# Attention with decay into a tanh MLP on one core: bulk loads unheld, first q copied at once, an early MLP start in slot 4, and unread matmuls in slots 0 to 3

## The chip, the cores and the metric

The kernel runs on 1 core of one Trainium2 chip. The metric is the device time of one execution in microseconds; the time quoted is the median of several runs.

## The reference

The attention has 8 batches, 8 heads, 576 tokens and head size 64. Its result, with the 8 heads side by side (512 channels), goes row by row through a two-layer MLP of width 2048.

```python
scores = scale * np.matmul(q, k.transpose(0, 1, 3, 2))
cum = np.cumsum(np.log(np.clip(f, 0.0001, 1.0)), axis=-1)
decay = cum[:, :, :, None] - cum[:, :, None, :]
scores = np.where(causal, -1000000000.0, scores + decay)
attn = softmax(scores)                       # over the last axis
x = np.matmul(attn, v).transpose(0, 2, 1, 3).reshape(B * S, H * D)
h = x @ w_in
out = (h - np.tanh(h)) @ w_out               # float32, 4608 x 512
```

## The kernel before, in words

**Slots.** The 64 heads are worked as 32 pairs (two heads of one batch, four pairs a batch). Slot p computes the scores of pair p, the values of pair p-1, and turns the result of pair p-2 or p-1 into the transposed layout XR (channels by tokens) that the MLP reads. `att_items(p)` writes out a slot: seven score tiles (`TILES`, numbered ti 0 to 6), and between them transposes of the next pair's q and k (`trans`, line 232, for batches 0 to 2; later batches are transposed by DMA), loads (`LOADS`, keyed by slot and tile), `values` (line 325 and the division L332 to L334) and `turn`. `turn` goes over TensorE and a ScalarE copy (L345, L346) in batch 0 and over two DMA transposes on SyncE's queue (L348, L350) in the others.

**The MLP** works on 9 blocks u of 512 tokens, each of 16 steps `mlp1` (hidden tile ft: four matmuls over the channel quarters ci, Tanh on ScalarE, the sum on VectorE; L360, L363, L366) and 16 steps `mlp2` (four matmuls each, L374; every fourth ends with a ScalarE copy and a store, L378 and L380). Channel quarter ci is pair ci of a batch. The list `mlp` of 288 steps is handed out to the slots, `take` of them to each (none in slots 0 to 3, then 2, 8, 7, 7, 7, 7, and 8 from slot 10 on), spread among a slot's items after the first `first` items; the remaining steps run behind slot 32.

**Scores.** A tile is a matmul of KT by QT over 64 rows of head dimension and 3 rows that add the decay: chi and clo (the scaled cumulative sum in two halves, rows of KT) and cq (a row of QT). These rows are put in place by DMA (`load_aug`). In the first pair, tiles 0 to 2 add the decay by two extra matmuls instead (`decay_part`, L263 and L265, from `dec`, `sel` and `cq`), so that they need no row from a DMA. Exp runs on ScalarE (L303). In batch 0 the causal mask is a further matmul (L297), in the others a GpSimd select (L313).

**The order of the work.** Inside `tc.manual_schedule` the instructions of TensorE, GpSimd, SyncE and VectorE run in the order in which the program writes them; ScalarE's order is left to a scheduler. Loads of q, k, v and the weights are issued on GpSimd's queue; decay rows, DMA transposes and stores mostly on SyncE's.

**The start.** q and k of heads 0 to 3 are loaded first, f gives lf (clip L140, Ln L148), cum (scan L150), chi (L153) and clo (L157). `start()` issues 33 unread matmuls (L389: products of a constant tile that nothing reads), transposes the first q and k, copies them out of PSUM (four ScalarE copies L243, four VectorE copies L245, two of each left over for `later()`), calls `load_aug(0)`, then `bulk()`, which loads heads 4 to 7 of q and k and the rest of v for batch 0. Ahead of that load stands `hold`: VectorE writes one column of clo into a place of qn that the load overwrites, so the load can't be issued before clo is there (L173).

**PSUM pools.** `ps_sc` has two buffers for score tiles, `ps_av` one for values, `ps_m` three (MLP, early transposes, `turn` of batch 0), `ps_tr` one (late transposes, score tile 3 in batch 0, and the unread matmuls).

Of the kernel before, what the change touches and what calls it, by code (L numbers as in the profile page):

```python
# [21 lines left out]
def kernel(  # L22
# [10 lines left out]
    nc = tc.nc  # L33
    P = 128

    B, H, S, D = q.shape
    NH = B * H
# [3 lines left out]
    NPAIR = H // 2  # L41
# [5 lines left out]
    NCH = DM // P  # L47
    UW = 512
    NU = NT // UW

    cst = ctx.enter_context(tc.tile_pool(name="cst", bufs=1))
# [9 lines left out]
    ps_tr = ctx.enter_context(tc.tile_pool(name="ps_tr", bufs=1, space=PSUM))  # L61
    ps_m = ctx.enter_context(tc.tile_pool(name="ps_m", bufs=3, space=PSUM))
# [61 lines left out]
    minus16 = cst.tile([2 * H, S], FP16)  # L124
    nc.vector.memset(minus16, -1.0)
    nc.vector.memset(sel, 0.0)
    nc.vector.memset(sel[0:1, 0:UW], -1.0)
    nc.vector.memset(sel[NH:NH + 1, 0:UW], -1.0)
    nc.vector.memset(sel[0:1, UW:UW + P], 1.0)
    nc.vector.memset(dec[:, S:PITCH], 0.0)  # L130
# [4 lines left out]
    late = cst.tile([P, P], FP16)  # L135
    nc.vector.memset(late, 0.0)
# [3 lines left out]
    nc.vector.tensor_scalar(out=lf, in0=lf, scalar1=0.0001, scalar2=1.0,  # L140
                            op0=ALU.max, op1=ALU.min)
    def clean(i, eng):
        eng.memset(KT[i][:, :, S:PITCH], 0.0)
        eng.memset(vn[i][D:P, NJ - 1, :, :], 0.0)
        eng.memset(vn[i][:, :, :, D:VW], 1.0)

    clean(0, nc.vector)
    nc.scalar.activation(out=lf, in_=lf, func=AF.Ln)  # L148
# [10 lines left out]
    def load_aug(b):  # L159
        i, hs = b % 2, slice(b * H, (b + 1) * H)  # L160
        nc.sync.dma_start(out=KT[i][D:D + 1, :, 0:S], in_=chi[hs, :])
        (nc.gpsimd if b == 0 else nc.sync).dma_start(out=QT[i][D + 2:D + 3, :, :], in_=cq[hs, :])
        nc.sync.dma_start(out=KT[i][D + 1:D + 2, :, 0:S], in_=clo[hs, :])

    def const_rows(i):
# [2 lines left out]

    const_rows(0)

    def hold(dst, *at):
        spot = dst[0][(slice(0, NH),) + at]
        nc.vector.tensor_copy(out=spot, in_=clo[:, 0:1])  # L173

    def bulk():
        hold(qn, 4, 0, slice(0, 1))
        load_qk(qn, q, 0, 4, H)
        load_qk(kn, k, 0, 4, H)
        for n in range(NJ - 1):
            load_v_block(0, n, 2, H)  # L180
# [156 lines left out]
    def turn(b, c):  # L337
        xn = XN.pop((b, c))
        r0 = b % 4 * S
        if b == 0:  # L340
            x32 = ps_m.tile([P, UW], FP32, tag="m", name="x32")
            xt = x32.bitcast(FP16)[:, 0:S]
            for ib in (NJ - 1, 0, 1, 2, 3):
                w0 = min(ib * P, S - P)
                nc.tensor.transpose(out=xt[:, w0:w0 + P], in_=xn[:, ib, :], identity=id16)  # L345
            nc.scalar.activation(out=XR[:, c, r0:r0 + S], in_=xt, func=AF.Copy)  # L346
            return
        nc.sync.dma_start_transpose(out=XR[:, c, r0:r0 + S - D].rearrange("p (n t) -> p n t", t=P),  # L348
                                    in_=xn[:, 0:NJ - 1, :].rearrange("p n d -> p (n d)"))
        nc.sync.dma_start_transpose(out=XR[:, c, r0 + S - D:r0 + S], in_=xn[D:P, NJ - 1, :])  # L350

    def mlp1(u, ft):
        hps = ps_m.tile([P, UW], FP32, tag="m", name="hps")
        t0 = u * UW % RING
        parts = [(0, t0, min(UW, RING - t0))]
        if t0 + UW > RING:
            parts.append((RING - t0, 0, t0 + UW - RING))
        for o, t, n in parts:
            for ci in range(NCH):
                nc.tensor.matmul(out=hps[:, o:o + n], lhsT=win[:, ci, ft * P:(ft + 1) * P],  # L360
                                 rhs=XR[:, ci, t:t + n], start=(ci == 0), stop=(ci == NCH - 1))
        th = tmp.tile([P, UW], FP32, tag="th", name="th")
        nc.scalar.activation(out=th, in_=hps, func=AF.Tanh, scale=-1.0)  # L363
        gt = gtp.tile([P, UW], FP16, tag="gt", name="gt")
        GT[(u, ft)] = gt
        nc.vector.tensor_tensor(out=gt, in0=hps, in1=th, op=ALU.add)  # L366
# [12 lines left out]
            r0 = u * UW + m * P  # L379
            nc.sync.dma_start(out=out[r0:r0 + P, :], in_=ost)  # L380

    IDLE = []

    def unread(n):
        if not IDLE:
            IDLE.append(ps_tr.tile([P, UW], FP32, tag="tr", name="idle"))
        idle = IDLE[0]
# [3 lines left out]
    pairs = [(b, c) for b in range(B) for c in range(NPAIR)]  # L391

    def start():
        unread(33)
        rest = trans(*pairs[0], qn, QT, True, "AAAA", True)
        nc.scalar.activation(out=cq, in_=cum, func=AF.Copy, bias=-SHIFT * inv_qscale, scale=inv_qscale)
        nc.scalar.activation(out=expo, in_=lf[0:1, 0:1], func=AF.Exp)
        load_aug(0)
        unread(6)
        rest += trans(*pairs[0], kn, KT, True, "VVVV", True)  # L400
        bulk()
        unread(12)
        decay(0)
        unread(8)
        REST.extend(rest)

    REST = []

    def later():
        for fn in REST:  # L410
# [10 lines left out]
    def att_items(p):  # L421
        def put(fn, *args):
            items.append((lambda: fn(*args), True))

        items = []
        here = pairs[p] if p < len(pairs) else None
        before = pairs[p - 1] if 0 < p <= len(pairs) else None
        after = pairs[p + 1] if p + 1 < len(pairs) else None
        early = p < NPAIR
        if p == 0:  # L430
            put(start)
        for ti in range(len(TILES)):
            if here:
                put(scores, *here, ti)
            if p == ti == 0:
                put(later)
            if p == 1 and ti == 3:
                put(last)
            for load in LOADS.get((p, ti), ()):
                items.append((load, False))  # L440
            if ti == 0 and after and after[0] < FAR:
                put(trans, *after, qn, QT, early, "VV")
            if ti == (1 if early else 3) and after and after[0] < FAR:
                put(trans, *after, kn, KT, early, "VV")
            if early and ti in (2, 3) and before:
                put(values, *before, (ti - 2,))
            elif not early and ti == 2 and before:
                put(values, *before)
            if p < NPAIR:
                if ti == 1 and p > 1:  # L450
                    put(turn, *pairs[p - 2])
            elif p == NPAIR and ti in (1, 5):
                put(turn, *pairs[p - 2 + (ti == 5)])
            elif p > NPAIR and ti == 3:
                put(turn, *before)
        return items

    mlp = [(fn, u, s) for u in range(NU) for fn in (mlp1, mlp2) for s in range(NFT)]
    at = 0
# [47 lines left out]
```

## Time and profile before

| what | value |
|---|---|
| median of 3 runs | 361.09 us (356.47 to 362.28) |
| the profiled execution: its time, its span | 361.41 us, 359.7 us |
| mean granted TensorE clock in the span | 0.986 |
| TensorE busy | 348.2 us, 97% |
| ScalarE, VectorE, GpSimd busy | 219.0, 197.4, 156.1 us |
| HBM read, written | 36.85 MB, 9.44 MB |
| share of TensorE in the chain that ended last | 86% |

How to read it: the span is what the profiler saw of one execution, the time is what the device reports for it. PE is TensorE's matmuls, PEld its weight loads, DVE VectorE, ACT ScalarE, POOL GpSimd, SP SyncE; SPq and POOLq are their instruction queues. L232 is line 232 of the kernel. The granted clock is a share of TensorE's full clock. Busy shares are means over the whole span; what a stage is worth is read from that stage.

### The profile page before, as it was taken

To read this page: it belongs to the slowest core of one execution; us is meant where nothing else is said; L and a number is where in the kernel's file an instruction comes from. 1 tells how busy PE (TensorE), PEld (TensorE's weight loads), DVE (VectorE), ACT (ScalarE), POOL (GpSimd) and SP (SyncE) were. 2 spreads that over 40 slices of the span, in tenths; PEclk is the share of its full clock that TensorE was granted. 3 is DMA by queue.
4 is the path that set the end of the run, shared out by engine and by line. 5 is a ranking of instruction groups with operands and counts; after the bars stand their busy time and mean duration, and the time that the engine had idled before them with its cause. 6 is when DMAs were issued, how large, how long until landed. Compare 5 with 4: busy or idle time off the path is not lost.

```text
span 359.7 us, 7576 instructions
## 1 busy us (share of the span) xinstructions
PE 348.2 (97%) x2833; PEld 194.3 (54%) x2833; DVE 197.4 (55%) x348; ACT 219.0 (61%) x417; POOL 156.1 (43%) x317
## 2 busy tenths in 40 slices
PE   7798999999999999999999999999999999999995
PEld 6486555555455555555557865555555544444442
DVE  8768897458871577157714681477137513802710
ACT  6559786467755785578557865786468634714611
POOL 7882743765376627662767267732222210000000
PEclk9859999999999999999999999999999999999999
DMA  9999999999499969997999999991320031011011
GB/s 109 133 206 193 181 186 141 141 130 163 70 82 179 164 93 80 170 154 116 76 127 190 112 73 142 150 156 18 91 67 13 19 88 61 2 58 58 2 48 69
DMA packets 140712, 38.74 MB, mean 108 GB/s; under 512 B 128084, under 2 KB 134980, under 8 KB 140676
## 3 DMA queue, kind: packets, MB, share of 16 engines
q0 software_dynamic: 92416, 18.37, 62.8%
q1 hardware_dynamic: 48260, 19.90, 28.4%
q8 instruction: 22, 0.36, 0.4%
q14 instruction: 14, 0.11, 0.1%
HBM read 36.85 MB, written 9.44 MB: 129 GB/s over the span
## 4 chain that ended last, share of the span: by engine, by line
PE 86%; DVE 5%; ACT 3%; DMA 3%; issue 1%; POOL 0%; POOLq 0%; ACTq 0%
PE ops L374 33%; PE hps L360 32%; PE ps L294 11%; PE av L325 8%; ACT e L303 3%; DMA kn<-in_k_dram 2%; DMA XR<-xn 1%; PE t L232 1%; DVE gt L366 1%; DVE KT L245 1%; PE ps L297 0%; DVE xn L334 0%; DVE QT L245 0%; ACT XR L346 0%; DVE cum L150 0%
## 5 line engine op out<-in xcount | busy, mean ns | idle before, releaser
L366 DVE TENSOR_TENSOR gt<-hps,th 128x512 f16<-128x512 f32 x144 | 98.5, 689 | 94.5 <-ACT th L363 93.7
L360 PE MATMUL hps<-XR,win 128*128 128x512 f16 (+1 forms) x640 | 140.2, 357 | 0.4 <-DVE gt L366 0.3
L374 PE MATMUL ops<-wout,gt 128*128 128x512 f16 x576 | 138.2, 379 | 0.0
L303 ACT ACTIVATE e<-ps 128x512 f16<-128x512 f32 x192 | 110.5, 598 | 27.6 <-PE ps L294 20.5
L363 ACT ACTIVATE th<-hps 128x512 f32<-128x512 f32 x144 | 86.7, 602 | 33.6 <-PE hps L360 31.0
L313 POOL TENSOR_SCALAR_AFFINE_SELECT e<-e 128x128 f16<-128x128 f16 x168 | 56.7, 338 | 87.7 <-ACT e L303 85.1
L360 PEld LDWEIGHTS <-win 128*128 128x128 f16 x640 | 58.0, 97 | 50.1 <-issue 1.3
L374 PEld LDWEIGHTS <-gt 128*128 128x128 f16 x576 | 52.2, 97 | 54.3
L294 PE MATMUL ps<-QT,KT 67*128 67x64 f16 (+5 forms) x384 | 78.3, 282 | 2.2 <-ACT e L303 1.7
L294 PEld LDWEIGHTS <-KT 67*128 67x128 f16 (+1 forms) x384 | 37.5, 99 | 37.6 <-issue 2.8
L378 ACT ACTIVATE ost<-ops 128x512 f32<-128x512 f32 x36 | 21.5, 596 | 50.8 <-PE ops L374 49.0
L325 PEld LDWEIGHTS <-e 128*128 128x128 f16 x896 | 33.4, 99 | 6.4 <-POOL e L313 0.7
L325 PE MATMUL av<-vn,e 128*128 128x65 f16 x896 | 34.9, 195 | 0.6 <-POOL e L313 0.6
L105 POOL DMA_DIRECT2D vn<-in_v_dram x32 | 27.9, 876 | 7.2 <-DMA win<-in_moe_w_in_dram 4.1
L334 DVE TENSOR_TENSOR xn<-av,rs 128x640 f16<-128x640 f32 x32 | 26.4, 825 | 1.1
L332 DVE TENSOR_SCALAR rs<-av 128x10 f32<-128x10 f32 x32 | 5.2, 162 | 34.9 <-PE av L325 34.6
L245 DVE COPY QT<-t 64x576 f16<-64x576 f16 x22 | 17.6, 802 | 10.9 <-PE t L232 10.7
L86 POOL DMA_DIRECT2D qn<-in_q_dram x25 | 21.4, 856 | 2.7 <-issue 2.7
L86 POOL DMA_DIRECT2D kn<-in_k_dram x25 | 21.1, 845 | 2.6 <-issue 2.6
L303 ACT ACTIVATE el<-ps 128x128 f16<-128x128 f32 x32 | 8.8, 276 | 21.6 <-PE ps L294 21.2
L313 POOL TENSOR_SCALAR_AFFINE_SELECT el<-el 128x128 f16<-128x128 f16 x28 | 8.3, 297 | 28.3 <-ACT el L303 28.1
L245 DVE COPY KT<-t 64x576 f16<-64x576 f16 (+1 forms) x26 | 19.4, 748 | 1.2 <-PE t L232 0.9
(62 smaller groups left out, 137.4 us busy)
## 6 DMA issues: line engine op xcount, KB each, us to landing
out_dram<-ost SPq DMA_DIRECT2D x36, 256.0 KB
vn<-in_v_dram POOLq DMA_DIRECT2D x24, 128.0 KB, 5.5
qn<-in_q_dram POOLq DMA_DIRECT2D x20, 128.0 KB, 3.7
kn<-in_k_dram POOLq DMA_DIRECT2D x20, 128.0 KB, 4.8
win<-in_moe_w_in_dram POOLq DMA_DIRECT2D x2, 1024.0 KB, 12.9
wout<-in_moe_w_out_dram POOLq DMA_DIRECT2D x2, 1024.0 KB, 11.6
XR<-xn SPq DMA_TRANSPOSE x56
vn<-in_v_dram POOLq DMA_DIRECT2D x12, 64.0 KB, 4.9
```

Source lines behind the costliest of these rows:

```text
L86: nc.gpsimd.dma_start(out=dst[b % 2][0:pn, n, :].rearrange("p (h d) -> p h d", h=H), in_=src[b, :, n * P:n * P + pn, :].rearrange("h p d - ...
L105: nc.gpsimd.dma_start(out=vn[b % 2][:, n, h0:h1, 0:D], in_=v[b, h0:h1, n * P:(n + 1) * P, :].rearrange("h p d -> p h d"))
L245: nc.vector.tensor_copy(out=to, in_=of)
L294: nc.tensor.matmul(out=ps[:, col:col + n], lhsT=KT[b % 2][0:rows, h, j * P:(j + 1) * P], rhs=QT[b % 2][0:rows, h, i0:i0 + n], start=not ow ...
L303: nc.scalar.activation(out=e[:, lo:hi], in_=ps[:, lo:hi], func=AF.Exp, scale=qscale)
L313: nc.gpsimd.affine_select(out=view, in_=view, compare_op=ALU.is_ge, fill=0.0, base=0, pattern=pat, channel_multiplier=-1)
L325: nc.tensor.matmul(out=av[:, a, ib, :], lhsT=E.pop((b, c, a, j, ib)), rhs=vn[b % 2][:, j, 2 * c + a, 0:D + 1], start=(j == 0), stop=(j == ib))
L334: nc.vector.tensor_tensor(out=xn.rearrange("p i (a d) -> p a i d", a=2), in0=av[:, :, :, 0:D], in1=rs.to_broadcast([P, 2, NJ, D]), op=ALU. ...
L360: nc.tensor.matmul(out=hps[:, o:o + n], lhsT=win[:, ci, ft * P:(ft + 1) * P], rhs=XR[:, ci, t:t + n], start=(ci == 0), stop=(ci == NCH - 1))
L363: nc.scalar.activation(out=th, in_=hps, func=AF.Tanh, scale=-1.0)
L366: nc.vector.tensor_tensor(out=gt, in0=hps, in1=th, op=ALU.add)
L374: nc.tensor.matmul(out=ops, lhsT=GT[(u, ft)][:, m * P:(m + 1) * P], rhs=wout[:, ft, :], start=(ft == 0), stop=(ft == NFT - 1))
```

## The change

Five groups of edits:

- **Start chain.** Of the two one-row memsets of -1 in `sel`, the one in row 64 becomes a ScalarE Copy (scale -1) of a row of ones. The memsets of `late` and of the end of `dec` move ahead of the remaining ones, and in `clean` the memset of KT moves behind those of vn. All of `start()` is now in written order on ScalarE too: two q copies, then cq, then Exp's first use, and the two other q copies between score tiles.
- **Bulk loads.** `hold` is gone, so `bulk()` depends on nothing. The cq row of batch 0 is loaded on SyncE's queue.
- **Slots 0 to 3.** `unread(3)` follows score tiles 0, 1, 2, 5 and 6. `unread` takes a new tile from `ps_tr` at each call; the call with 12 in the start now has 22. Score tiles 0 and 1 of the first pair are part of `start()`, and the transposes of pair 1 move to tiles 1 (q) and 3 (k) of slot 0.
- **Slot 4.** `turn` of pair 2 follows tile 0; after tile 1 come the values of pair 3, then three `mlp1` steps over channel quarters 0 to 2 alone, then the turn of pair 3 (through `ps_tr`); their last quarter, Tanh and sum follow tiles 2 to 4. Its transposes move to tiles 2 and 4.
- **Handing out.** The three steps leave the list; slots take 2 (slot 4), 7 (5 to 7), 6 (slot 8) and 8 (from slot 9 on).

```diff
-    nc.vector.memset(sel[NH:NH + 1, 0:UW], -1.0)
+    nc.scalar.activation(out=sel[NH:NH + 1, 0:UW], in_=ones16[0:1, 0:UW], func=AF.Copy, scale=-1.0)
...
     def load_aug(b):
-        (nc.gpsimd if b == 0 else nc.sync).dma_start(out=QT[i][D + 2:D + 3, :, :], in_=cq[hs, :])
+        nc.sync.dma_start(out=QT[i][D + 2:D + 3, :, :], in_=cq[hs, :])
...
-    def hold(dst, *at):
-        spot = dst[0][(slice(0, NH),) + at]
-        nc.vector.tensor_copy(out=spot, in_=clo[:, 0:1])
-
     def bulk():
-        hold(qn, 4, 0, slice(0, 1))
         load_qk(qn, q, 0, 4, H)
...
-            x32 = ps_m.tile([P, UW], FP32, tag="m", name="x32")
+            x32 = (ps_tr if c == NPAIR - 1 else ps_m).tile([P, UW], FP32, tag="tr" if c == NPAIR - 1 else "m", name="x32")
...
-    def mlp1(u, ft):
-        hps = ps_m.tile([P, UW], FP32, tag="m", name="hps")
+    HP = {}
+
+    def mlp1(u, ft, part=None):
+        if part != 1:
+            HP[(u, ft)] = ps_m.tile([P, UW], FP32, tag="m", name="hps")
+        hps = HP[(u, ft)]
...
-            for ci in range(NCH):
+            for ci in {None: range(NCH), 0: range(NCH - 1), 1: (NCH - 1,)}[part]:
...
+        if part == 0:
+            return
...
     def start():
         unread(33)
-        rest = trans(*pairs[0], qn, QT, True, "AAAA", True)
+        q_rest = trans(*pairs[0], qn, QT, True, "AAAA", True)
...
         load_aug(0)
         unread(6)
-        rest += trans(*pairs[0], kn, KT, True, "VVVV", True)
+        k_rest = trans(*pairs[0], kn, KT, True, "VVVV", True)
         bulk()
-        unread(12)
+        unread(22)
         decay(0)
         unread(8)
-        REST.extend(rest)
...
+        scores(*pairs[0], 0)
+        for fn in k_rest:
             fn()
+        q_rest[0]()
+        scores(*pairs[0], 1)
+        q_rest[1]()
...
-            if here:
+            if here and (p > 0 or ti > 1):
                 put(scores, *here, ti)
+            if early and ti in (0, 1, 2, 5, 6):
+                put(unread, 3)
...
-            if ti == 0 and after and after[0] < FAR:
+            at_q, at_k = (1, 3) if p == 0 else (0, 1) if early else (2, 4) if p == NPAIR else (0, 3)
+            if ti == at_q and after and after[0] < FAR:
                 put(trans, *after, qn, QT, early, "VV")
-            if ti == (1 if early else 3) and after and after[0] < FAR:
+            if p == NPAIR and ti > 1 and ti < 5:
+                put(mlp1, 0, ti - 2, 1)
+            if ti == at_k and after and after[0] < FAR:
                 put(trans, *after, kn, KT, early, "VV")
-            if early and ti in (2, 3) and before:
+            if p == NPAIR:
+                if ti == 0:
+                    put(turn, *pairs[p - 2])
+                elif ti == 1:
+                    put(values, *before)
+                    for ft in range(3):
+                        put(mlp1, 0, ft, 0)
+                    put(turn, *before)
+            elif early and ti in (2, 3) and before:
...
-    with tc.manual_schedule(engines={PE, mybir.EngineType.Pool, mybir.EngineType.SP, mybir.EngineType.DVE}):
+    with tc.manual_schedule(engines=FOUR | {mybir.EngineType.Activation}):
+        start()
+    with tc.manual_schedule(engines=FOUR):
...
-            take = 0 if p < NPAIR else 2 if p == NPAIR else 7 if NPAIR + 1 < p <= 2 * NPAIR + 1 else 8
+            take = 0 if p < NPAIR else 2 if p == NPAIR else 7 if p < 2 * NPAIR else 6 if p == 2 * NPAIR else 8
-            first = 10 if p == NPAIR else 0 if p == NPAIR + 1 else 0
+            first = 16 if p == NPAIR else 0
```

More of the change, by code (lines that the diff above doesn't have):

```diff
@@ L126 @@
     nc.vector.memset(sel, 0.0)
+    late = cst.tile([P, P], FP16)
+    nc.vector.memset(late, 0.0)
+    nc.vector.memset(dec[:, S:PITCH], 0.0)
     nc.vector.memset(sel[0:1, 0:UW], -1.0)
-    nc.vector.memset(sel[NH:NH + 1, 0:UW], -1.0)
     nc.vector.memset(sel[0:1, UW:UW + P], 1.0)
-    nc.vector.memset(dec[:, S:PITCH], 0.0)
+    nc.scalar.activation(out=sel[NH:NH + 1, 0:UW], in_=ones16[0:1, 0:UW], func=AF.Copy, scale=-1.0)
     EL = [cst.tile([P, 192], FP16, tag=f"el{i}", name=f"el{i}") for i in range(3)]
@@ L134 @@
     load_v_head(0, 1)
-    late = cst.tile([P, P], FP16)
-    nc.vector.memset(late, 0.0)
     nc.gpsimd.affine_select(out=late, in_=late, compare_op=ALU.is_ge, fill=-60000.0,
@@ L142, in clean @@
     def clean(i, eng):
-        eng.memset(KT[i][:, :, S:PITCH], 0.0)
         eng.memset(vn[i][D:P, NJ - 1, :, :], 0.0)
         eng.memset(vn[i][:, :, :, D:VW], 1.0)
+        eng.memset(KT[i][:, :, S:PITCH], 0.0)
     clean(0, nc.vector)
@@ L380, in mlp2 @@
             nc.sync.dma_start(out=out[r0:r0 + P, :], in_=ost)
-    IDLE = []
     def unread(n):
-        if not IDLE:
-            IDLE.append(ps_tr.tile([P, UW], FP32, tag="tr", name="idle"))
-        idle = IDLE[0]
+        idle = ps_tr.tile([P, UW], FP32, tag="tr", name="idle")
         for i in range(n):
@@ L391 @@
     pairs = [(b, c) for b in range(B) for c in range(NPAIR)]
+    REST = []
     def start():
         unread(33)
-        rest = trans(*pairs[0], qn, QT, True, "AAAA", True)
+        q_rest = trans(*pairs[0], qn, QT, True, "AAAA", True)
         nc.scalar.activation(out=cq, in_=cum, func=AF.Copy, bias=-SHIFT * inv_qscale, scale=inv_qscale)
@@ L399, in start @@
         unread(6)
-        rest += trans(*pairs[0], kn, KT, True, "VVVV", True)
+        k_rest = trans(*pairs[0], kn, KT, True, "VVVV", True)
         bulk()
-        unread(12)
+        unread(22)
         decay(0)
         unread(8)
-        REST.extend(rest)
-    REST = []
-    def later():
-        for fn in REST:
-            fn()
+        scores(*pairs[0], 0)
+        for fn in k_rest:
+            fn()
+        q_rest[0]()
+        scores(*pairs[0], 1)
+        q_rest[1]()
         for e in EL[0:2]:
@@ L429, in att_items @@
         early = p < NPAIR
-        if p == 0:
-            put(start)
         for ti in range(len(TILES)):
-            if here:
+            if here and (p > 0 or ti > 1):
                 put(scores, *here, ti)
-            if p == ti == 0:
-                put(later)
+            if early and ti in (0, 1, 2, 5, 6):
+                put(unread, 3)
             if p == 1 and ti == 3:
@@ L451, in att_items @@
                     put(turn, *pairs[p - 2])
-            elif p == NPAIR and ti in (1, 5):
-                put(turn, *pairs[p - 2 + (ti == 5)])
             elif p > NPAIR and ti == 3:
@@ L458 @@
     mlp = [(fn, u, s) for u in range(NU) for fn in (mlp1, mlp2) for s in range(NFT)]
+    mlp = mlp[3:]
     at = 0
-    with tc.manual_schedule(engines={PE, mybir.EngineType.Pool, mybir.EngineType.SP, mybir.EngineType.DVE}):
+    FOUR = {PE, mybir.EngineType.Pool, mybir.EngineType.SP, mybir.EngineType.DVE}
+    with tc.manual_schedule(engines=FOUR | {mybir.EngineType.Activation}):
+        start()
+    with tc.manual_schedule(engines=FOUR):
         for p in range(len(pairs) + 1):
```

## The prediction

> **What bounds the kernel now.** I read the page first: busy time and slices, then the chain.
>
> ```profile
> PE 348.2 (97%) x2833; PEld 194.3 (54%) x2833; DVE 197.4 (55%) x348; ACT 219.0 (61%) x417; POOL 156.1 (43%) x317
> PE   7798999999999999999999999999999999999995
> PEclk9859999999999999999999999999999999999999
> PE 86%; DVE 5%; ACT 3%; DMA 3%; issue 1%; POOL 0%; POOLq 0%; ACTq 0%
> ```
>
> TensorE sets the end nearly everywhere. From about 40 us it is full at full clock, and no edit removes work there. Room is left only in the first slices, where TensorE is less busy and the third slice has half the clock. Second view: the first 40 us in stretches of 1 us (busy time of PE, PEld, DVE, ACT, POOL, then granted clock, DMA share, GB/s).
>
> ```profile
> 9.00:10.00 1.00, 1.00 (x15) 0.62 (x12) 0.92 (x4) 0.45 (x2) 0.51 (x1) 1.00 0.09 15
> 10.00:11.00 1.00, 1.00 (x9) 0.34 (x6) 0.97 (x4) 0.43 (x1) 1.00 (x3) 1.00 0.23 41
> ...
> 15.00:16.00 1.00, 0.59 (x7) 0.24 (x4) 0.79 (x2) 0.96 (x3) 1.00 (x2) 0.94 2.31 158
> 16.00:17.00 1.00, 0.00 (x0) 0.00 (x0) 0.80 (x1) 0.23 (x1) 0.17 (x1) 0.50 2.39 154
> ...
> 26.00:27.00 1.00, 1.00 (x27) 0.88 (x25) 0.66 (x2) 0.10 (x1) 0.16 (x1) 0.94 1.11 211
> ```
>
> The reader sees an unused DMA at 9 to 11 us, an empty TensorE at 16 us, and the half clock from 15.88 to 26.12 (0.94 is 12% of a microsecond at half). Third: the timelines of GpSimd and TensorE name the cause.
>
> ```profile
> 9.49 0.71 POOL L80 DMA_DIRECT2D qn<-in_q_dram  x1 [1.25 <-DVE qn L173]
> 10.18 0.67 POOL L80 DMA_DIRECT2D kn<-in_k_dram  x1
> ...
> 17.03 0.66 PE L232 MATMUL t<-id,kn 96*128 96x96 f16 x6 [1.44 <-DMA kn<-in_k_dram]
> ```
>
> The held load of k is issued at 10.18 and lands 6.8 us later, while TensorE stands for 1.44 us. The slots (one head pair each) begin with their first 512-wide score matmul at 9.25, 14.46, 22.01, 28.32 and 32.94 (slot 4), and slot 5 at 39.35. The change must bring slot 4's start and slot 4 itself forward.
>
> **The change, part by part.**
>
> *Start chain.* One memset (3.48 to 4.02, 0.54 us) leaves VectorE's queue ahead of the clip, the scan and the first scores. ScalarE writes that row by a Copy ahead of Ln. Here is the unknown:
>
> ```profile
> 0.81 1.28 ACT L148 ACT_TABLE_LOAD   x1 [0.81 <-PEq L491]
> 4.61 0.68 ACT L148 ACTIVATE lf<-lf 64x576 f32<-64x576 f32 x1 [2.52 <-DVE lf L140]
> 5.31 1.28 ACT L397 ACT_TABLE_LOAD   x1
> ```
>
> Loads stand where a function first needs one, so the Copy, now first, may get a load of its own and push Ln's behind it: memset of sel done 2.70, Copy about 0.6, load 1.28, Ln 4.63 to 5.31, against 5.29 now. Then the scan comes 0.1 us earlier instead of 0.54. I take 0.1 (ends 0 and 0.54), so the first scores start at 9.15. The q copies move ahead of cq and of Exp's load; that load then ends near 8.9, before the first Exp near 9.75. If the scores came 0.9 us earlier it would be late.
> The Trainium skill (ScalarE: Activation LUTs, Table sets: the hidden batching unit) says that cheap functions are in every set as filler; by that alone Ln's set could serve the Copy and the gain would be 0.54. No run so far has a Copy before Ln.
>
> *Bulk loads.* Without the hold GpSimd goes on at 7.36 (end of its select L137) instead of 9.49, 2.1 us earlier; the DMA share from 9 to 12 is 0.35, so 3 x 0.65 = 1.95 us of transfer time lie unused there. I take 1.8: k lands at 15.2. TensorE will reach the transposes that need it at about 15.9 (below): the 1.44 us wait goes. The first half of win, landing at 29.98, comes at 28.2; slot 4 will want it near 30.5, so it stays covered. The cost: batch 0's three decay rows (SyncE, 0.66 us of issue each, cq's now also there, so 7.2 to 9.2) share the engines with bulk traffic. The rows of batch 1, issued 10.09 to 12.17 beside bulk traffic, have their packets on the engines up to 16, up to 4.4 us after issue. So the last row lands by 13; the fourth tile of slot 0 wants it at about 12.7. I take 0.2 us of loss (ends 0 and 1.5).
>
> *Unread matmuls.* Ten more in the start are covered by the wait for clo (now 1.2 us). In slots 0 to 3 there are 15 each at 0.058 us (12 take 0.70 us at full clock): 0.87 us. What hides them: slot 3, at full clock, lasts 4.62 us, and its TensorE timeline stands for 0.23 + 0.63 + 0.15 = 1.0 us, because ScalarE (0.27 to 0.6 per exponential plus 0.65 for XR) and VectorE (1.61 + 1.62 + 0.17 + 0.22 + 0.83 = 4.45 us) set the pace. Uncovered they would cost 0.87 us a slot. Their tile has one buffer, shared with the fourth score tile, so the fourth group waits for that tile's Exp; the scores just ahead already wait for an earlier Exp, hence nothing.
> What they buy is the clock. It rises between the transposes at 4.83 (0.66 us for six, half rate) and at 5.79 (0.42), falls at 15.88 and rises at 26.12: steps of 10.24 us. I count columns times rows/128 from TensorE's timeline. Whole steps don't separate (10431 before the fall, 8309 before the rise), thirds do: those before a full clock have 3352 (22.70 to 26.12) or more, those before a half clock 2735 (12.47 to 15.88) or less. Fifteen unread matmuls add 1920 columns a slot, about 1400 a window: 4100. The clock then holds.
> The Trainium skill (TensorE: Matmul & The Clock Gate, Why this matters for your kernels) asks only for no idle gap over about 3 us; the trace fell after 0.3 us of idling inside a 1.44 us gap, so it disagrees. By the rule the clock would owe nothing to the unread matmuls, and they would be a cost of up to 4 x 0.87 us, near rival 2's time.
>
> *Slots 0 to 3, summed.* Slot 0 lasts 5.21 us, of it 0.50 waiting for ScalarE; plus 0.87 less 0.50 gives 5.6 (the two q copies moved in here cost ScalarE 1.0 us, in 2.2 us that it stands there now): slot 1 at 14.75, its k transposes near 15.9. Three slots at 4.65 (slot 3's pace): slot 4 at 28.7 instead of 32.94. Gain 4.2 us, the start chain's 0.1 within it.
>
> *Slot 4.* It takes 6.41 us now. Its work at full clock: two MLP pieces 1.74, values 0.91, two turns 0.56, transposes 0.52, scores 1.38, together 5.1; 1.3 us is waiting for XR, VectorE and ScalarE. The three part-pieces (9 matmuls, 1.94 us) lie just where values' division (1.3 us) must be waited for. Three more whole pieces are done here, work and not gain. ScalarE then has 7.7 us in a slot of about 8, so I take 1.0 (ends 0.3 and 1.3).
>
> *Given back at slot 9.* The MLP is two steps further on, so the first piece of token block 1, which needs pair 7's XR, comes first in slot 9. Now:
>
> ```profile
> 73.98 1.29 SPq L348 DMA_TRANSPOSE XR<-xn  x1
> ...
> 77.67 1.24 PE L360 MATMUL hps<-XR,win 128*128 128x512 f16 x4
> ```
>
> The transfer takes 4.50 us in the chain and costs TensorE 0.2 us. From the last value matmul (71.78) it is issued after 2.2 us, or 1.55 where no store is ahead (pair 6: 62.85, 64.39): landing after 6.05. TensorE gets there after 0.2 + three MLP steps of 0.865 + scores 0.72 + transposes 0.26 + 0.65 of the piece = 4.45. Wait 1.6, 0.2 of it there already; I take 1.2 net (ends 0 and 1.6). What is late next: nothing, the other engines catch up. At the later blocks five steps lie between (about 6.1 us), nothing by the same landing.
>
> **Sum.** 4.2 - 0.2 + 1.0 - 1.2 = 3.8 us off the profiled execution's own 361.41 (its span 359.7 and 1.7 around it): 357.6. That execution is 0.3 above the median 361.09, so 357.3.
>
> **Rivals.**
> 1. *More gain.* Ln is not pushed back (0.45 more), the transfer lands in time at slot 9 (1.2), slots at VectorE's 4.5 us (0.45), slot 4 full (0.3): 354.9. For it: each is an end above, and one run of 356.47 exists. Against: VectorE and ScalarE must interlock perfectly.
> 2. *The clock falls all the same* in slots 1 to 3: 10.24 us at half rate, where a slot's 8094 columns (scores 3200, masks 1152, values 1950, transposes 1152, turn 640) and 1920 unread ones at half rate (0.104 us per 128, from 33 weight loads in 3.44 us) take 8.1 us: 1.26 slots instead of 2.2, 4.4 us lost, giving 361.7. For it: the count above rests on few windows. Against: 4100 is far above 3352.
> 3. *Slower: the decay rows queue behind the bulk.* If they pass only with k's bulk load, TensorE stands in slot 0 from 12.7 to about 17 (4.3 us), the clock falls there (4.2 more): 365.8. It decides once the rows land after 16.5. For it: that is what the hold prevented. Against: batch 1's rows passed bulk traffic in 4.4 us or less.
> 4. *XR late at all block starts.* If landing takes 1 us more, slots 9, 13, 17, 21 and 25 each lose 1: 362.3. For it: those slots have block loads on the engines. Against: only one such wait is in the chain now.
>
> **Chances and range.** Main forecast 0.52 (by itself 355.5 to 359.5), rivals 0.20, 0.13, 0.08, 0.07. Range 353.4 to 361.8: left out are the lower part of 1, half of 2, all of 3 and much of 4, about 0.2. Two per cent is 7.2 us, about what a measurement of this kernel can tell from no change. Faster by that (under 353.9): half of rival 1, 0.10. Slower (over 368.3): half of rival 3, 0.04. Within: 0.86.
>
> **What would show it.** Right: clock 1.00 in every stretch from 7 us on; no TensorE wait for k's load; q's bulk issue near 7.4; a third table load; slot 4 starting near 28.7; a TensorE wait of about 1.4 us for XR near slot 9. Wrong: half clock in slots 1 to 3, a wait for KT or QT rows in slot 0, or slots of over 5 us with VectorE waiting for TensorE.

## The result, and the profile after

The changed kernel takes 372.62 us (median of 4 runs, 369.69 to 373.59), the kernel before beside it 359.05 us (356.47 to 362.28): ratio 1.0389, interval 1.027 to 1.0508. It is slower by some 14 us; 357.3 had been forecast, with 361.8 as the upper end. The profiled execution took 373.59 us, its span is 371.9 us and the mean granted clock 0.991. The kernel before has the half clock of its profile only in some executions: beside the experiments below, those at a granted clock of 0.997 or more take 356.8 to 359.1 us, those at 0.986 take 360.6 to 363.2.

First the page of the changed kernel: busy time, slices of TensorE and its clock, and the shares of the chain.

```profile
PE 351.2 (94%) x2903; PEld 195.2 (52%) x2903; DVE 199.9 (54%) x346; ACT 222.9 (60%) x419; POOL 156.1 (42%) x316
...
PE   7898999969999899989998999899999999999995
...
PEclk9999899998999999999999999999999999999999
...
PE 78%; DMA 8%; DVE 8%; ACT 4%; issue 2%; SPq 0%; POOLq 0%; POOL 0%; ACTq 0%
```

TensorE's busy time rose only from 348.2 to 351.2 us, while its share of the span fell from 97% to 94%: the loss is mostly waiting. The slices show where. Where before had nines from the fifth slice on, the ninth slice now has a 6, and the 14th, 18th, 22nd and 26th have an 8, regularly four slices apart. The clock dips in the fifth slice (slot 4) and the tenth (slot 9). DMA has 8% of the chain instead of 3%. The list of TensorE's waits names the transfer (us in total, times, longest):

```profile
PE hps L359 <- DMA XR<-xn: 9.3, 5, 2.9
PE ps L289 <- ACT e L298: 1.2, 5, 0.3
...
PE t L227 <- DVE QT L240: 0.9, 1, 0.9
...
PE ps L289 <- PE idle L386: 0.7, 1, 0.7
```

Five waits for XR take 9.3 us. (The last line is the wait of slot 0's fourth tile at 13.85 us, the first that needs the decay rows; the unread matmul that it names was long done, and other profiles put the same wait down to the cq row.) The timeline of TensorE has them at the first piece of a token block, here the first two:

```profile
81.55 0.38 PE L359 MATMUL hps<-XR,win 128*128 128x512 f16 x1 [2.90 <-DMA XR<-xn]
...
123.92 0.38 PE L359 MATMUL hps<-XR,win 128*128 128x512 f16 x1 [1.63 <-DMA XR<-xn]
```

The chain has the transfers themselves, from issue to landing, of pairs 7, 11, 15 (and 19, 23 likewise):

```profile
75.48 6.02 DMA XR<-xn
...
118.40 5.48 DMA XR<-xn
...
157.05 5.41 DMA XR<-xn
```

They take 5.4 to 6.0 us where the chain of before had 4.5. I laid the two traces over each other at equal progress, that is where the same matmul columns are done, unread ones not counted. The changed kernel is 1.6 us behind in slot 0, 2.5 ahead at the end of slot 3 (slot 4 starts at 30.57 instead of 32.94), up to 3.4 ahead within slot 4, and level at the start of slot 5. Then it loses 4.5 us at slot 9 and about 1.75 at each of slots 13, 17, 21 and 25; with 0.4 between, the sum at the end is 12.3 us. So there are three questions: why XR is late, what eats the gain of slot 4, and why slots 0 to 3 brought 2.5 us instead of 4.2.

### The profile page after: what moved, and what is told of

Read it like the earlier page. It is cut to its first block, busy times and chain, and to the rows that moved or that the text cites. A ratio compares the mean times of both kernels' runs of the same rounds, so it can differ in the third digit from the quotient of the medians.

```text
span 371.9 us, 7713 instructions
## 1 busy us (share of the span) xinstructions
PE 351.2 (94%) x2903; PEld 195.2 (52%) x2903; DVE 199.9 (54%) x346; ACT 222.9 (60%) x419; POOL 156.1 (42%) x316
## 4 chain that ended last, share of the span: by engine, by line
PE 78%; DMA 8%; DVE 8%; ACT 4%; issue 2%; SPq 0%; POOLq 0%; POOL 0%; ACTq 0%
PE hps L359 30%; PE ops L375 28%; PE ps L289 10%; DMA XR<-xn 8%; PE av L320 7%; DVE gt L367 2%; DVE QT L240 2%; DVE KT L240 2%; PE t L227 1%; ACT e L298 1%; DVE xn L329 1%; ACT ost L379 1%; PE idle L386 1%; ACT th L364 0%; PE ps L292 0%
## 5 line engine op out<-in xcount | busy, mean ns | idle before, releaser
L359 PE MATMUL hps<-XR,win 128*128 128x512 f16 (+1 forms) x640 | 143.5, 362 | 9.3 <-DMA XR<-xn 9.3
L289 PE MATMUL ps<-QT,KT 67*128 67x64 f16 (+5 forms) x384 | 77.4, 279 | 2.4 <-ACT e L298 1.2
L320 PEld LDWEIGHTS <-e 128*128 128x128 f16 x896 | 32.5, 98 | 6.7 <-POOL e L308 0.9
L320 PE MATMUL av<-vn,e 128*128 128x65 f16 x896 | 34.0, 193 | 0.8 <-POOL e L308 0.8
L386 PE MATMUL idle<-warm 128*128 128x128 f16 x129 | 12.6, 239 | 1.2 <-DVE warm L113 1.1
```

The lines of the kernel that those rows point to most:

```text
L289: nc.tensor.matmul(out=ps[:, col:col + n], lhsT=KT[b % 2][0:rows, h, j * P:(j + 1) * P], rhs=QT[b % 2][0:rows, h, i0:i0 + n], start=not ow ...
L320: nc.tensor.matmul(out=av[:, a, ib, :], lhsT=E.pop((b, c, a, j, ib)), rhs=vn[b % 2][:, j, 2 * c + a, 0:D + 1], start=(j == 0), stop=(j == ib))
```

## The experiments

The accounts weighed in the expectations are: the hand-out, two MLP steps further on, runs into the XR transfers (theory A), which the k loads stretch (F); slot 4's new order costs by itself (E); the unheld loads delay the decay rows, and the clock with them (C, C2); the unread matmuls lengthen the slots (G). Ratios are to the kernel before, run beside each; a tenth of a per cent is 0.36 us.

### XR: hand-out or transfer

**back2**: the changed kernel with two steps fewer handed out ahead of slot 9.

```diff
-            take = 0 if p < NPAIR else 2 if p == NPAIR else 7 if p < 2 * NPAIR else 6 if p == 2 * NPAIR else 8
+            take = {4: 2, 5: 7, 6: 7, 7: 6, 8: 6, 9: 7}.get(p, 8 if p > 9 else 0)
```

> The changed kernel with its hand-out two MLP steps later (38 steps given by the end of slot 9, 46 by slot 10, as before the change). Theory A (XR too late: the two-step shift puts the first piece of token blocks 1 to 5 first in slots 9, 13, 17, 21, 25, ahead of the DMA transpose that it reads): the waits for XR fall from 9.3 us to under 1, the half clock behind slot 9 goes, about 11 us off: 361 to 363. Theory B (the transposes are late because of earlier or other traffic in the changed kernel, wherever the pieces stand): waits stay over 5 us, 367 or more.

Measured: 365.6 us (365.36 to 367.11), ratio 1.0218 (1.0179 to 1.0257). TensorE's waits in its trace:

```profile
PE hps L359 <- DMA XR<-xn: 1.8, 1, 1.8
```

The four later waits are gone, so they do hang on the two steps. The one at slot 9 stays, because slots 7 and 8 hand out 6 steps each here: between the last values of pair 7 and the first piece of the block lies one step fewer than before. A half-clock stretch from 81.77 to 85.19 follows it, and so the time missed the 361 to 363 us that theory A gave.

**back1**: the same with one step fewer.

```diff
+            take = {4: 2, 5: 7, 6: 7, 7: 7, 8: 5, 9: 8}.get(p, 8 if p > 9 else 0)
```

> The changed kernel with its hand-out one step later. Theory A: the wait is landing minus arrival, and arrival moves by one step of 0.87 us, so each of the four waits of 1.75 falls to about 0.9 and the one at slot 9 from 3.1 to about 2.2: 366 to 369. Theory B: no dose, 371 or more, or all gone at once.

Measured: 368.32 us (365.59 to 369.28), ratio 1.0273 (1.0217 to 1.0329). Three XR waits remain, 2.7 us together; a 2.1 us wait for the cq row in slot 0 and half clock from 17.31 to 24.14 came on top in its profile. By the waits, one step takes off more than two thirds of the 9.3 us.

**ahead2**: the other way round, the kernel before with two steps more.

```diff
-            take = 0 if p < NPAIR else 2 if p == NPAIR else 7 if NPAIR + 1 < p <= 2 * NPAIR + 1 else 8
+            take = {4: 2, 5: 8, 6: 8, 7: 8, 8: 6, 9: 8}.get(p, 8 if p > 9 else 0)
```

> The kernel before with nothing changed but its hand-out, now two steps ahead from slot 8 on (32 steps by the end of slot 8, 40 by slot 9). Theory A: it alone costs 8 to 11 us: 367 to 371, with five waits for XR. Theory B: within 2 us of before, no waits.

Measured: 371.39 us (368.8 to 372.68), ratio 1.0362 (1.0305 to 1.042). TensorE's waits in its trace:

```profile
PE hps L360 <- DMA XR<-xn: 8.0, 5, 3.2
```

Nothing of the change but the hand-out is in this kernel, and nearly the whole loss is there: the same five waits, and behind the longest half clock from 80.11 to 83.53. It keeps the hold, the old slot 4 and no unread matmuls in slots 0 to 3; none of these is needed for the loss.

**k_earlier**: the changed kernel, hand-out and all, with the k loads of each later batch (small packets, GpSimd's queue) issued one slot earlier.

```diff
-            LOADS.setdefault((p0, n), []).append(lambda b=b, n=n: load_block(kb, k, b, n))
+            LOADS.setdefault((p0 - 1, n), []).append(lambda b=b, n=n: load_block(kb, k, b, n))
```

> The changed kernel with k's block loads (batches 3 to 7) one slot earlier, so that they don't run beside the turn of a batch's last pair. Theory F (their traffic stretches that DMA transpose from issue to landing to 5.4 to 6.0 us): it lands in under 4 us, the waits for XR fall from 9.3 to under 4: 364 to 368. Rival (it is late for other reasons: the store ahead of it on SyncE's queue, the q transposes behind it): 371 to 374.

Measured: 364.88 us (363.88 to 366.56), ratio 1.016 (1.0096 to 1.0224). One XR wait of 0.2 us is left among TensorE's waits (a wait of 1.8 us for the cq row in slot 0 stands there too), and its chain has one XR transfer:

```profile
77.01 3.35 DMA XR<-xn
```

That is 3.35 us instead of 6.02. The packet records say why: the 512 packets of the larger transpose of these pairs are done 3.5 to 4.0 us after issue in the changed kernel, 2.3 to 2.8 here, and 2.0 for pairs 27 and 31, which have no block loads beside them. So the hand-out makes XR's landing decide, and the k loads on the same DMA engines make it late. Either cure takes most of the waits away: 1.8 us are left in back2, 0.2 here.

### The start: rows, hold, unread matmuls

**slot4_old**: the changed kernel with slot 4 and the hand-out as before.

```diff
-            first = 16 if p == NPAIR else 0
+            first = 10 if p == NPAIR else 0
...
-    mlp = mlp[3:]
...
+            elif p == NPAIR and ti in (1, 5):
+                put(turn, *pairs[p - 2 + (ti == 5)])
```

> The changed start and slots 0 to 3 (unheld loads, ScalarE copies, unread matmuls) with slot 4 and the hand-out as before the change. Theory A with the progress seen in the trace (2.5 us ahead at the end of slot 3): about 2.5 under a run of before that has the half clock, 355.5 to 358.5, no half clock in the first 40 us. Rival: slot 4 as such gives the 2.5 us back (it waits for something else that starts no earlier): 359 to 361.

Measured: 362.55 us (361.34 to 364.11), ratio 1.0139 (1.0092 to 1.0186). It is slower than before and above both accounts. TensorE's timeline in slot 0:

```profile
14.72 0.19 PE L289 MATMUL ps<-QT,KT 67*128 67x64 f16 x1 [1.60 <-DMA QT<-cq]
```

The fourth tile stands for the cq row, and half clock follows from 17.07 to 20.49.

**slot4_old_held**: the same with `hold` back and the cq row on GpSimd's queue.

```diff
+        hold(qn, 4, 0, slice(0, 1))
...
-        nc.sync.dma_start(out=QT[i][D + 2:D + 3, :, :], in_=cq[hs, :])
+        (nc.gpsimd if b == 0 else nc.sync).dma_start(out=QT[i][D + 2:D + 3, :, :], in_=cq[hs, :])
```

> As slot4_old, but the bulk loads held for clo again and cq's row on GpSimd's queue ahead of them. Theory C (unheld bulk traffic keeps the decay rows of batch 0 on their way until 13.8 to 15.2 us; TensorE stands 0.7 to 2.1 us for them in slot 0 and may lose the clock): that wait goes, the wait of 1 to 1.4 us for k comes back, the unread matmuls keep the clock: 357 to 360, 3 to 5 under slot4_old's 362.6. Rival D (the unread matmuls and the rest of the start cost it, not the loads): 361.5 or more.

Measured: 358.85 us (358.49 to 359.66, 10 runs), before 359.67; ratio 0.9987 (0.9952 to 1.0021), clock 0.998 or more in every run. The row wait went, but the wait for k that was expected back did not come: k's load goes out at 10.25, as before, and TensorE reaches the transposes that need it only at 16.63 (before stood there from 15.59 to 17.03) and does not wait. The time is within the forecast, and no gain over before shows; this run doesn't tell whether unread matmuls bridge a gap.

**unheld**: the kernel before without `hold` and with nothing else; the cq row stays on GpSimd's queue, ahead of the bulk.

```diff
-        hold(qn, 4, 0, slice(0, 1))
```

> The kernel before with only the hold taken out (cq's row still on GpSimd's queue ahead of the bulk loads). Theory C: k's wait goes, the rows chi and clo land late, TensorE waits for them in slot 0 by 0.5 to 2 us and the clock falls as before: 359 to 363 against 358.6 for before. Rival (the loads were a gain that other edits ate): 1 to 2 us faster than before, no wait for rows in slot 0.

Measured: 356.77 us (356.24 to 361.57, 10 runs); ratio 0.9953 (0.9914 to 0.9993). The 359 to 363 us that one account gave did not come. There is no row wait in the trace and the clock is 1.00 without any unread matmul in slots 0 to 3: the progress is 5.0 us ahead at the end of slot 3, twice what the change as a whole has there. That is against a profile of before with 10.24 us of half clock; by the ratio the gain is 0.5%. One of the ten runs has a granted clock of 0.991 and 361.57 us. GpSimd's timeline:

```profile
7.68 0.55 POOL L162 DMA_DIRECT2D QT<-cq  x1 [0.33 <-ACT cq L391]
8.23 0.71 POOL L80 DMA_DIRECT2D qn<-in_q_dram  x1
```

The bulk of q goes out at 8.23 instead of 9.49, behind cq. So it is not wholly free here: it waits for cq, where in the changed kernel it goes out at 6.83.

**slot4_old_cqpool**: slot4_old with the cq row on GpSimd's queue (the line shown above), the loads unheld.

> As slot4_old, loads unheld, but cq's row of batch 0 on GpSimd's queue ahead of the bulk loads. Theory C2 (what costs slot 0 its wait is that row on SyncE's queue behind unheld bulk loads, since the kernel before with only the hold removed showed no such wait): no wait for QT in slot 0, clock 1.0 in nearly all runs, 355.5 to 358 against slot4_old's 362.6. Rival (the bulk loads starting at 6.8 delay chi and clo just as much): 360 or more.

Measured: 359.04 us (358.49 to 361.17, 10 runs); ratio 1.0003 (0.9972 to 1.0034). The row wait is gone and the clock stays at 0.997 or more: against slot4_old 1.4% or 4.9 us by the ratios, 3.5 by the medians, for one line (in the profile of slot4_old a wait of 1.6 us and 3.4 us of half clock). That line does two things: it moves the row to the other queue, and it makes the bulk loads wait for cq, so that q's goes out at 8.28 instead of 6.83. Which of the two frees the rows was not tried apart. The forecast of 355.5 to 358 missed. What is left of slots 0 to 3's loss is seen in TensorE's timeline:

```profile
24.67 0.33 PE L386 MATMUL idle<-warm 128*128 128x128 f16 x3 [0.63 <-ACT el L298]
```

Unread matmuls wait 0.63 us for the Exp of the fourth tile, with which they share the one buffer, and the scores behind them wait too.

**cqpool_nounread**: the same without the unread matmuls of slots 0 to 3.

```diff
-            if early and ti in (0, 1, 2, 5, 6):
-                put(unread, 3)
```

> As slot4_old_cqpool without the 15 unread matmuls in each of slots 0 to 3. Theory G (where no transfer opens a gap the clock holds without them, and they lengthen a slot from 4.6 to 4.95 us): 1 to 1.7 us under slot4_old_cqpool, 354.3 to 356.3. Rival (they are what holds the clock): half clock in slots 1 to 3 in several runs, 358 or more.

Measured: 357.77 us (356.43 to 359.53, 7 runs); ratio 0.994 (0.9905 to 0.9974), clock 0.994 or more. Slots 1 to 3 take 4.11, 4.61 and 4.62 us instead of 4.59, 5.28 and 4.95, and at slot 4 it is 5.0 us ahead of before, instead of 2.66 with them. So the unread matmuls cost 2.35 us there; 0.8 of it goes again at slot 9, where TensorE now waits 1.5 us for XR instead of 0.7. Over the whole kernel they cost 2.3 us by the ratios and 1.3 by the medians of the two, run side by side; the forecast time of 354.3 to 356.3 missed. The clock hardly needs them, since the gap that pulled it down, the wait for k, is gone already: it is under 0.995 in 4 of the 29 runs of unheld, cqpool_nounread and unheld_k (below), which leave them out of slots 0 to 3, and in none of the 20 of slot4_old_held and slot4_old_cqpool, which have them.

**after_cqpool**: the changed kernel with the cq row on GpSimd's queue.

> The changed kernel with that one line undone (cq's row on GpSimd's queue ahead of the bulk loads). Theory C2: the row wait of 0.7 to 2.1 us goes and nothing else; the waits for XR stay: 368.5 to 371.5. Rival (the loss is all in the XR waits): 372 to 373.

Measured: 371.56 us (370.12 to 372.77); ratio 1.0333 (1.0287 to 1.0379). XR waits 8.4 us. The time is just above the 368.5 to 371.5 expected: the row is a small part of the whole loss.

### Slot 4

The timeline of TensorE of the changed kernel in slot 4:

```profile
35.70 0.41 PE L227 MATMUL t<-id,qn 96*128 96x96 f16 x6 [0.52 <-ACT XR L341]
...
37.91 0.42 PE L227 MATMUL t<-id,kn 96*128 96x96 f16 x6 [0.86 <-DVE QT L240]
```

The three part-pieces hold all of `ps_m`, so the turn of pair 3, the transposes of q and those of k pass one after another through the one buffer of `ps_tr`; q's wait for the copy of XR that empties it and k's for those of QT. VectorE's timeline of the same kernel shows a second account:

```profile
36.16 1.61 DVE L240 COPY QT<-t 64x576 f16<-64x576 f16 x2 [2.08 <-PE t L227]
37.79 2.11 DVE L367 TENSOR_TENSOR gt<-hps,th 128x512 f16<-128x512 f32 x3
39.82 1.60 DVE L240 COPY KT<-t 64x576 f16<-64x576 f16 x2
```

VectorE stands for 2.08 us and then works without a break. The sums of the three MLP pieces lie between q's copies and k's, so KT is ready only at 41.42, some 3 us after k's transposes.

**back2_q0**: back2 with the q transposes of slot 4 moved ahead of the turn.

```diff
-            at_q, at_k = (1, 3) if p == 0 else (0, 1) if early else (2, 4) if p == NPAIR else (0, 3)
+            at_q, at_k = (1, 3) if p == 0 else (0, 1) if early else (0, 4) if p == NPAIR else (0, 3)
```

> As back2, but in slot 4 the transposes of the next q come after tile 0 instead of tile 2, so that the one buffer of ps_tr passes from them to the turn of pair 3 and then to k, with work between. Theory E (in slot 4 turn, q and k queue for that buffer: 0.7, 1.0 and 1.0 us of TensorE gaps): those gaps shrink to about 1 us in all, 363.5 to 365 against 365.6. Rival (ScalarE and VectorE are simply full there): same time.

Measured: 365.43 us (362.42 to 366.69), ratio 1.0183 (1.0114 to 1.0252), not to be told from back2. Both gaps shown above went, and others came: 0.52 us for XR's copy at 35.71 and 1.05 us for KT's copies at 40.66, which start behind the three sums. Same time is what the rival gave (ScalarE and VectorE simply full), which speaks against the one buffer as the whole cause.

**repaired**: the changed kernel with the cq row on GpSimd's queue and the k loads a slot earlier; slot 4 and hand-out as changed.

> The changed kernel with cq's row on GpSimd's queue and k's block loads one slot earlier. Theories A, C2 and F together: no wait for XR or rows is left; what remains against slot4_old_cqpool is slot 4's order, 2 to 3 us: 358.5 to 361. If it is not over slot4_old_cqpool, slot 4's loss was the clock and not the order.

Measured: 362.09 us (361.63 to 363.05, 8 runs); ratio 1.0071 (1.0037 to 1.0105). No XR wait and no row wait is left in the list; against slot4_old_cqpool 0.68% or 2.4 us stay (3.1 by the medians), and the time is above the 358.5 to 361 of the forecast. Its profile has half clock from 38.17 to 41.59, behind slot 4's gaps, but its five runs at a granted clock of 1.00 take 361.6 to 362.3 us just the same: the loss is not the clock.

**unheld_k** and **unheld_k_slot4**: unheld with the k loads a slot earlier, and the same with the change's slot 4 and hand-out.

> The kernel before with the hold taken out and k's block loads one slot earlier. Theory: with the old hand-out XR is hardly waited for (0.4 us in unheld), so the loads bring 0 to 0.4 us: 356.0 to 357, under before in most runs. If block loads matter beyond XR's transposes it is under 355.5.

> As unheld_k with slot 4 and the hand-out of the change. Theory E (slot 4's order costs by itself: turn, q and k transposes pass one buffer one after the other while three part-pieces hold the other three): 2 to 3 us over unheld_k, 358.3 to 360, with the same gaps of 0.7, 1.0 and 1.0 us in slot 4. Rival (it costs only where slots 0 to 3 arrive late or with unread matmuls): within 0.8 of unheld_k.

Measured: unheld_k 356.98 us (356.85 to 364.56, 12 runs; before 359.64), ratio 0.9934 (0.99 to 0.9967); unheld_k_slot4 359.89 us (359.53 to 364.86), ratio 1.0002 (0.9965 to 1.0039). TensorE's timeline of the second, at full clock:

```profile
35.53 0.42 PE L227 MATMUL t<-id,kn 96*128 96x96 f16 x6 [0.86 <-DMA vn<-in_v_dram]
...
39.09 0.39 PE L289 MATMUL ps<-QT,KT 67*128 67x512 f16 x1 [0.83 <-DVE KT L240]
```

The same gaps stand in slot 4 although neither clock nor rows are disturbed, and XR only by 0.5 us at slot 9. (The first is put down to a load of v by the profile; it has the place and the length of the one put down to QT's copies in the changed kernel.) The second is a wait for KT's copies themselves, not for a buffer. All gaps of slot 4 add up to 2.7 us here and to 0.6 in unheld_k, and by equal progress 2.0 us are lost by 41 us. VectorE is busy for 6.37 of the 6.59 us from 33.77 on. So slot 4 and its hand-out cost 2.4 us by the ratios, 2.9 by the medians, and some 2 of that is slot 4's order by itself. unheld_k is faster than both kernels by its ratio, 0.7% below before; that the earlier k loads add to unheld's 0.5% doesn't show.

### The ledger

Ratios times 359.5 us, step by step; each step is one edit except the third, which also puts the k loads back into their slot (with the old hand-out they make little difference: unheld 0.9953, unheld_k 0.9934):

| step | ratio from, to | us |
|---|---|---|
| changed kernel, cq row to GpSimd's queue | 1.0389, 1.0333 | 2.0 |
| k loads a slot earlier: XR waits and the half clock behind the longest | 1.0333, 1.0071 | 9.4 |
| slot 4, hand-out and k loads as before | 1.0071, 1.0003 | 2.4 |
| no unread matmuls in slots 0 to 3 | 1.0003, 0.9940 | 2.3 |
| what is left: the loads unheld, and the start chain | 0.9940, 1 | -2.2 |

Each step has an uncertainty of about 0.5% (1.8 us), the first one of over 1%, since the changed kernel's own ratio is the widest; by the medians the third is 3.1 us and the fourth 1.3. unheld alone has 0.9953, so the start chain adds nothing that shows.

## Why the prediction was wrong, point by point

**The step that failed most: "At the later blocks five steps lie between (about 6.1 us), nothing by the same landing", and at slot 9 "I take 1.2 net".** The mechanism was named, with its place, and four of its five places were costed at nothing. Two terms were mis-sized. The transfer, taken at the 4.50 us of one row, lasts 5.4 to 6.0, because the k loads share the engines; and from the last value matmul to the issue it is 2.2 us at the later blocks, where a store is ahead on SyncE, instead of 1.55. At slot 9 the cover was right (4.7 us against 4.45) and the issue too (1.55); the transfer alone took the wait from 1.6 to 2.9. At the later blocks the cover was exact, 6.1 us, and the longer transfer was there to be read: in the trace of before its last packet comes 4.3 to 5.6 us after issue for pairs 11, 15, 19 and 23, against 4.2 for pair 7, the one row that was used. SyncE's timeline of the changed kernel shows the later issue for pair 11, whose last value matmul starts at 116.18 and whose division ends at 117.70:

```profile
117.95 0.34 SPq L381 DMA_DIRECT2D out_dram<-ost  x1
118.40 1.82 SPq L343 DMA_TRANSPOSE XR<-xn  x1
```

Landing is thus 2.2 + 5.4 = 7.6 us after the last values, against 6.1 us of cover: 1.5, where 1.6 was measured. Rival 4 (five blocks lose 1 us each) was the true picture at too small a price: 9.3 us of waits, and the half clock behind the first. It had 0.07, because "only one such wait is in the chain now": but that wait of 0.2 us said that no slack was left at slot 9, nothing was worked out for the slack at the other four, and the change takes away two steps of cover, 1.7 us. That the loads stretch the transfer is shown by k_earlier; how much the store ahead costs by itself was not tried.

**Clock.** "What is late next: nothing" missed that a 2.9 us wait empties a window and that the next 3.41 us then run at half clock, 1.7 us more at slot 9.

**Slot 4, "I take 1.0 (ends 0.3 and 1.3)".** Wrong in sign: 2.4 us lost. The 1.3 us of waiting was got by subtraction; in the trace of before TensorE is busy for 5.72 of the slot's 6.41 us and its waits there add up to 0.6, so there was less to win than was taken. I summed matmuls and divisions and did not ask which buffer each product needs, nor when VectorE can copy it out. With three part-pieces in `ps_m`, three products queue for one buffer of `ps_tr`; two of the gaps are waits for the copy that empties it (0.5 and 0.9 us), the third (0.8) is a wait for KT's copies behind VectorE's sums. That reading rests on the waits in the traces. Which of the two, the buffer or the full VectorE, is worth how much stays open: no experiment with a second buffer or another order of the copies was made.

**Unread matmuls, "hence nothing".** Wrong: 2.35 us up to slot 4, 1.3 to 2.3 over the kernel. The 0.87 us a slot are hidden only in part (pitch 4.95 us instead of the 4.65 of the sum, and in slot 0 next to nothing is hidden), and the shared buffer makes the fourth group wait 0.63 us, the very wait that I had waved off. In this profile the clock did hold through slots 0 to 3, as forecast; in those of back1, k_earlier and slot4_old, with the same start, it fell for 3.4 to 6.8 us behind a row wait of 1.6 to 2.1 us in spite of them. And it mostly holds without them (unheld, cqpool_nounread). The prediction bought the clock twice: with the k wait gone, the dip had lost its cause.

**The base.** The 4.2 us were priced on a profiled execution with 10.24 us of half clock, and many executions of before don't have it. unheld is 4.7 us ahead of that profile at the end and 0.5% faster by the ratio: over its executions the start could bring less than the sum took.

**Bulk loads: gain right, decay rows mis-sized.** The q bulk goes out at 6.83 (7.4 forecast), the k wait is gone. The 1.95 us of unused transfer time took a share of 1.00 for full, while the prediction's own rows reach 2.39; k's load went out at 7.51 instead of 10.18, and that was enough. For the rows "I take 0.2 us of loss (ends 0 and 1.5)": the waits were 0.7 to 2.1 us in five of the six profiles with this start, and half clock stands behind three of them. The cq row, issued on SyncE at 7.98, had its packets on the engines at 12 to 13; on GpSimd's queue, ahead of the bulk, its last packet is through 1.3 to 2.0 us after issue. Rival 3 was the mechanism, far milder than its 4.3 us.

**Start chain: right in its mechanism, and no gain.** ScalarE's timeline of the changed kernel:

```profile
0.81 1.28 ACT L132 ACT_TABLE_LOAD   x1 [0.81 <-PEq L500]
2.72 0.63 ACT L132 ACTIVATE sel<-ones 1x512 f16<-1x512 f16 x1 [0.63 <-DVE sel L126]
3.37 1.28 ACT L148 ACT_TABLE_LOAD   x1
4.66 0.68 ACT L148 ACTIVATE lf<-lf 64x576 f32<-64x576 f32 x1
...
7.46 1.28 ACT L396 ACT_TABLE_LOAD   x1
```

The Copy got a load of its own and Ln ends at 5.34, against 5.29 before; the scan follows at 5.38 (5.34 before), and the first scores start at 9.28 where 9.15 was forecast and 9.25 was before. The Trainium skill (ScalarE: Activation LUTs, Table sets: the hidden batching unit) has cheap functions in every set; here the trace shows that this did not spare the load.

**The sum,** by the progress of the two profiles: 4.2 - 0.2 became 2.5 at the start of slot 4, +1.0 became -2.5 (level at slot 5), and -1.2 became -12.3 from slot 9 on, drift included. The range ended at 361.8 because the landing at the later blocks had no bounds of its own: its price was that of a single transfer.

## What to carry to other kernels

When work is brought forward, look up every wait that it now meets earlier: where a transfer has a wait of even 0.2 us in the profile, its slack is zero there, and each transfer of the same form at the other blocks needs a sum from its own rows. Before more products are put in flight, count the buffers and look at the order of the engine that empties them, not only at the engines' time. Before a gain is priced on one profiled execution, ask how many executions have what it cures. When a stall is removed, ask whether the cures for its after-effects (here the unread matmuls) still have anything to cure.

## What the runs showed of the hardware

**The clock changed in windows of 3.41 us and followed the work done in them.** TensorE's view by stretches, cut here at the changed kernel's own clock steps (length, then busy time of PE, PEld, DVE, ACT, POOL, then granted clock, DMA share, GB/s):

```profile
34.89:38.31 3.42, 2.04 (x23) 1.10 (x21) 2.11 (x3) 2.88 (x6) 1.67 (x4) 1.00 1.42 189
38.31:41.72 3.41, 3.41 (x12) 1.43 (x10) 3.24 (x6) 2.17 (x4) 1.38 (x4) 0.50 1.21 189
79.26:82.68 3.42, 1.14 (x11) 0.65 (x11) 0.09 (x1) 0.60 (x1) 1.11 (x2) 1.00 1.95 155
82.68:86.09 3.41, 3.41 (x19) 1.69 (x18) 2.81 (x5) 1.73 (x4) 1.18 (x2) 0.50 0.83 152
```

After each of these thin windows the next is at 0.50 for 3.41 us. I counted matmul columns times rows/128 in such windows over all 16 profiles. Of the 16 windows that were followed by half clock, 15 have 3070 or less and one has 3214; all that were followed by full clock have 2955 or more. Between these the two overlap, so no sharp bound shows; the prediction's (between 2735 and 3352) holds, and is now narrower. The window from 34.89 has 3070 and fell: 1.4 us of gaps were enough. Idling alone does not describe it: the window of before from 19.29 to 22.70 is busy for 3.26 of 3.41 us at half clock, has 2701 columns, and half clock followed.

**Small transfers are stretched by loads on the same engines.** A 9 KB row had its last packet through 4.5 to 5.1 us after issue on SyncE's queue, beside bulk loads that started at 6.83, and 1.3 to 2.0 us on GpSimd's queue, ahead of bulk loads that then started near 8.3; the runs don't part the queue from the later start. An XR transpose's 512 packets took 2.0 us alone and 3.5 to 4.0 us beside the k loads.
